# Four sums and three low parts moved from POOL to DVE at two stage boundaries, and the last stage's second g tile loaded a step ahead into kept buffers

## The chip, the cores and the metric

One Trainium2 chip, one core. The metric is device microseconds of one execution. The kernel before takes 1404.5 us, the median of three runs (1402.43 to 1406.67).

## The reference, cut to what matters

```python
# B, H, S, D = 8, 8, 576, 64; tokens = 4608
k_p, v_p = mean of k, v over 8 keys
attn = softmax(q @ k_p.T / sqrt(D)) @ v_p            # -> x [4608, 512]
h  = x @ w_in                                        # [4608, 1024]
ln = layernorm(h * softmax(h)) * g_ln
x2 = ln @ w_out                                      # [4608, 512]
g  = silu(x2 @ w2_in)                                # [4608, 2048]
out = g @ w2_out                                     # [4608, 512]
```

All data are float32 and the weights come as 8-byte words. A product is made from two parts of each factor, a high part (rounded to fp32r by ACT) and a low part (what is left, by a subtraction): high*high, high*low and low*high, so three matmuls for each one.

## The kernel before, in words

The work has three stages.

**Lead-in** (0 to about 640 us): attention and the first FFN, in 36 token tiles of 128. A script of letters (`STEP`, and `TAIL` for the last tiles) sets the order on PE. For a token tile, `hidden1` (L440) makes h in PSUM, `solu_max` (L451, DVE) takes the row maximum, `solu_norm` the exponentials (L458, ACT) and their product with h (L459, DVE; L462, POOL), `solu_scale` the squares (L468, ACT), a chain of one-column instructions (L469 to L474, POOL) and the normalised row `e` (L475, POOL). `norm_T` transposes `e` on PE (L490) and splits it into `lnh` (L123, ACT) and `lnl` (L124, DVE), and `project1` (L510) makes x2, which goes through ACT (L513) to DRAM.

**Second FFN, first product** (from 614 us; the last tiles of the lead-in run beside its first call): one level of Strassen, 7 products in place of 8. There are 12 steps n (6 groups of 768 tokens, twice, for the halves of w2_in's columns) with 4 calls `hidden2(n, i)` each. A call makes 7 products of 6 matmuls (L707), in the order L11, S2, S1, S3, L12, S4, L22, and ACT (L723, L727, L736, L677), DVE (L717) and POOL (L717) put them together into `gt`, which SP stores to DRAM (L678). Token sums `T1` to `T4` and the split of tokens are made by `tokens(n)` (sums by `sub`, L529; high parts L640, ACT; low parts L529, DVE), weight sums and splits of quarter q by `quad(q)` (first sum L554 and the others L529, DVE; high parts L565, ACT; low parts L529, on DVE or, where `lo` is given `pool`, on POOL). `tokens(0)` and `quad(0)` come from the background queue of the lead-in. The products of call (0, 0) land in PSUM tiles of the lead-in; the fifth and the sixth share one tile of two banks.

**Last stage** (from 1020.86 us): g @ w2_out, again Strassen. A g tile q is 512 tokens by 512 of g's columns (1 MB in two row halves, 36 of them); `load_g` (L801, SP) reads it, `sums_g` (L811 and L529, POOL) makes two sums, `prepare(m)` one operand (high part L830, ACT; low part L529, DVE) into a ring of 9, and `product2` (L853) one block of 12 matmuls, 7 blocks to a g tile. So blocks 0 to 6 need the first g tile, 7 to 13 the second, 14 to 20 the third. The weights of part u come by `load_part(u, j)` (L785), issued on ACT's queue: part 0 for blocks 0 to 6 and half of the next seven, part 1 for the other half, parts 2 and 3 at blocks 4 and 11.

From step n = 0 of the second stage on, ACT, DVE, POOL and SP run in the order of the program; before that only PE does, and a scheduler orders the others. `plan` hangs pieces on 28 slots of a step, one after each product. In step 11, slot 0 loads the first g tile, the slots 1 to 24 hold the loads of parts 0 and 1, slot 10 `sums_g(0)`, and 14 to 27 `prepare(0)` to `prepare(6)`. `finish_pair` stores a call's `gt` in the next call, and the last one after the step. A DMA also waits, on its issuing queue, until the DMA eight issues earlier in the program has landed, since the program uses eight DMA semaphores in turn.

Buffers: pools on the "left" side are a stack. `wx` (2 buffers of 4 KB a partition) holds quarter sums and, from step 2 to 10, row buffers of w2_out (`load_rows`); `wr` holds the raw quarters (`w2r`). `wq1`, `to` and `wx` are closed after step 11 (`bt.close()`), and `gr1`, `gr2` and others open in their place.

```python
    load_g(1)          # L1112, behind bt.close()
    load_g(2)
    ...
    sums_g(1, s_tmp)
    prepare(7)()
    prepare(8)()
```

Of the kernel before, what the change touches and what calls it, by code (L numbers as in the profile page):

```python
# [9 lines left out]
F32 = mybir.dt.float32  # L10
# [15 lines left out]
P = 128  # L26
# [14 lines left out]
GO = 512  # L41
# [41 lines left out]
def pooled_attention__solu__silu_kernel(  # L83
# [13 lines left out]
    nc = tc.nc  # L97
# [422 lines left out]
    pools = {}  # L520
# [14 lines left out]
    wq, w2r = {}, {}  # L535
# [36 lines left out]
    def quad(q):  # L572
        sum_, hi, lo, src = quarter(q)
        pool = nc.gpsimd
        return [
# [51 lines left out]
    def tokens(n):  # L627
# [22 lines left out]

        eng = nc.gpsimd
        work = [
# [136 lines left out]
    def load_g(q):  # L789
        c, s = divmod(q, NSET)  # L790
        if q % 3 == 0:
            raw = pools["x2r"].tile([P, 2, 2, GO], F32, tag="x2r", name="gr")
        else:
            raw = pools[f"gr{q % 3}"].tile([P, 2, 2, GO], F32, tag="gr", name="gr")
        done = 0
        while done < GO:
            g, o = divmod(c * GO + done, G2)
            m = min(GO - done, G2 - o)
            for h in range(2):
                f = h * FC2 // 2 + 2 * s  # L800
                nc.sync.dma_start(raw[:, h, :, done : done + m], gd[g][:, f : f + 2, o : o + m])  # L801
            done += m
        graw[q] = raw
# [3 lines left out]
    def sums_g(q, temps):  # L807
        raw = graw[q]
        a11, a21, a22 = raw[:, 0, :, :256], raw[:, 0, :, 256:], raw[:, 1, :, 256:]
        s1, s2 = (temps(k).rearrange("p (f d) -> p f d", d=256) for k in (1, 2))  # L810
# [4 lines left out]
    def prepare(n):  # L815

        q, j = divmod(n, 7)
        raw = graw[q]
        a11, a21, a12, a22 = (raw[:, i, :, 256 * k : 256 * k + 256] for i in range(2) for k in range(2))
        s1, s2 = sums[q]  # L820
# [225 lines left out]
    )  # L1046
    banks[:] = [0]
    open_pool("wq1", 1, "left", bt)
    open_pool("to", 1, "left", bt)
    open_pool("wx", 1, "left", bt)  # L1050
    ctx.enter_context(
# [8 lines left out]
    for n in range(N2):  # L1060
# [22 lines left out]
        if n == N2 - 1:  # L1083
# [5 lines left out]
            ]  # L1089
            work = [(0, lambda: load_g(0))]  # L1090
            for j in range(7):
                work += [(3 * j + 1, lambda j=j: load_part(0, j, early[j], nc.scalar)),
                         (3 * j + 6, lambda j=j: load_part(1, j, more[j], nc.scalar))]
            s0 = lambda k: pools["wx"].tile([P, 512], F32, tag=f"a{k - 1}", name="s")
            lows = {}
# [13 lines left out]
    bt.close()  # L1109
    for name in ("gr1", "gr2", "ob", "m2", "w2o"):  # L1110
        open_pool(name, 1, "left")
    load_g(1)  # L1112
    load_g(2)

# [65 lines left out]
```

## Time and profile before

| | |
|---|---|
| runs, us | 1406.67, 1404.5, 1402.43 (median 1404.5) |
| the profiled execution, us | 1403.74 |
| its span, us | 1402.0 |
| PE busy (matmuls) | 1294.8 us, 92% |
| DVE / ACT / POOL busy | 71% / 51% / 47% |
| mean DMA rate | 162 GB/s |
| chain that ended last, by engine | PE 49%, DVE 7%, issue 5%, DMA 4%, ACT 3%, POOL 2% |

The span is the time from the first to the last instruction that the profile shows, on the one core that runs; the execution's own time is 1.74 us longer. The profile gives each instruction its start and duration, and the idle time of its engine just before it with what ended that. In the stages PE is the engine that is nearly always busy, so what is to be looked for are the places where it is not.

### The profile page before, as it was taken

To read this page: it belongs to the slowest core of one execution; us is meant where nothing else is said; L and a number is where in the kernel's file an instruction comes from. 1 tells how busy PE (TensorE), PEld (TensorE's weight loads), DVE (VectorE), ACT (ScalarE), POOL (GpSimd) and SP (SyncE) were. 2 spreads that over 40 slices of the span, in tenths; PEclk is the share of its full clock that TensorE was granted. 3 is DMA by queue.
4 is the path that set the end of the run, shared out by engine and by line. 5 is a ranking of instruction groups with operands and counts; after the bars stand their busy time and mean duration, and the time that the engine had idled before them with its cause. 6 is when DMAs were issued, how large, how long until landed. Compare 5 with 4: busy or idle time off the path is not lost.

```text
span 1402.0 us, 23904 instructions
## 1 busy us (share of the span) xinstructions
PE 1294.8 (92%) x8712; PEld 1227.4 (88%) x8712; DVE 999.4 (71%) x1438; ACT 709.1 (51%) x1772; POOL 661.5 (47%) x829
## 2 busy tenths in 40 slices
PE   2589899999999999889998999999979999999998
PEld 2469789988989899789888988999979999999998
DVE  6896566766766565445787889888547788877785
ACT  4684555565555555343554555554433444434442
POOL 5674344444444433444555666777323333433332
PEclk7899999999999999999999999999989999999999
DMA  7655244543434211122566678665776344444431
GB/s 227 207 159 164 80 130 143 156 139 114 140 99 128 91 61 61 61 76 94 194 243 250 245 266 307 238 237 195 294 271 255 128 151 151 151 129 143 134 95 74
DMA packets 100550, 227.01 MB, mean 162 GB/s; under 512 B 8272, under 2 KB 29776, under 8 KB 98896
## 3 DMA queue, kind: packets, MB, share of 16 engines
q1 hardware_dynamic: 96400, 210.80, 45.1%
q10 hardware_dynamic: 4032, 14.68, 2.8%
q8 instruction: 69, 1.13, 0.3%
q14 instruction: 49, 0.40, 0.1%
HBM read 141.56 MB, written 83.89 MB: 161 GB/s over the span
## 4 chain that ended last, share of the span: by engine, by line
PE 49%; DVE 7%; issue 5%; DMA 4%; ACT 3%; POOL 2%; SPq 0%; ACTq 0%; DVEq 0%; POOLq 0%
PE op L853 24%; PE m L707 12%; PE xp L510 6%; PE hp L440 5%; DVE gt L717 2%; DVE wr L529 1%; PE tp L490 1%; DMA w2r<-w2if 1%; DVE t L529 1%; DVE u L717 1%; ACT gt L677 1%; DMA x2r<-x2d 1%; PE sp L311 1%; DMA w2o<-wod 1%; DVE w2r L529 1%
## 5 line engine op out<-in xcount | busy, mean ns | idle before, releaser
L707 PE MATMUL m<-t,w2s 128*128 128x384 f32 x2016 | 367.2, 340 | 23.9 <-DVE gt L717 11.8
L707 PEld LDWEIGHTS m<-t,w2s 128*128 128x128 f32 x2016 | 352.4, 190 | 38.3 <-DVE gt L717 14.6
L853 PE MATMUL op<-w2o,gt 128*128 128x256 f32 x3024 | 368.0, 284 | 8.5 <-ACT gt L830 7.9
L853 PEld LDWEIGHTS op<-w2o,gt 128*128 128x128 f32 x3024 | 366.0, 193 | 10.5 <-ACT gt L830 8.8
L529 DVE TENSOR_TENSOR gt<-gr,gt 128x512 fp32r<-128x512 f32 x180 | 164.7, 949 | 67.4 <-ACT gt L830 67.4
L830 ACT ACTIVATE gt<-gr 128x512 fp32r<-128x512 f32 x180 | 103.2, 623 | 151.4 <-DVE gr L529 132.5
L717 POOL TENSOR_TENSOR gt<-u,m 128x384 f32<-128x384 f32 x96 | 114.5, 1203 | 134.3 <-ACT m L727 91.8
L510 PE MATMUL xp<-lnh,w1oh 128*128 128x256 f32 x576 | 168.1, 292 | 0.5 <-ACT lnh L123 0.2
L510 PE MATMUL xp<-lnl,w1oh 128*128 128x256 f32 x576 | 163.9, 285 | 1.1 <-DVE lnl L124 1.1
L510 PE MATMUL xp<-lnh,w1ol 128*128 128x256 f32 x576 | 163.8, 284 | 0.0
L440 PE MATMUL hp<-w1ih,xTh 128*128 128x512 f32 x288 | 119.0, 413 | 8.9 <-DVE e L459 8.9
L736 ACT ACTIVATE gt<-gt 128x768 f32<-128x768 f32 x48 | 40.7, 847 | 157.2 <-DVE gt L717 157.2
L811 POOL TENSOR_TENSOR s<-gr 128x512 f32<-128x512 f32 x36 | 58.3, 1618 | 127.1 <-DVE gt L529 74.2
L329 ACT ACTIVATE pr<-sp,st 128x72 f32<-128x72 f32 x288 | 88.3, 330 | 56.8 <-POOL st L321 56.7
L440 PE MATMUL hp<-w1il,xTh 128*128 128x512 f32 x288 | 115.5, 401 | 0.6 <-POOL w1il L156 0.6
L440 PE MATMUL hp<-w1ih,xTl 128*128 128x512 f32 x288 | 115.7, 402 | 0.3 <-DVE xTl L124 0.3
L510 PEld LDWEIGHTS xp<-lnh,w1oh 128*128 128x128 f32 x576 | 111.4, 193 | 1.7 <-DVE lnl L124 0.7
L510 PEld LDWEIGHTS xp<-lnl,w1oh 128*128 128x128 f32 x576 | 111.6, 194 | 1.4 <-DVE lnl L124 1.3
L510 PEld LDWEIGHTS xp<-lnh,w1ol 128*128 128x128 f32 x576 | 111.3, 193 | 0.0
L529 DVE TENSOR_TENSOR t<-tt,t 128x768 fp32r<-128x768 f32 x48 | 64.8, 1354 | 14.1 <-ACT t L640 14.0
L440 PEld LDWEIGHTS hp<-w1ih,xTh 128*128 128x128 f32 x288 | 56.3, 196 | 21.1 <-issue 9.2
L830 ACT ACTIVATE gt<-s 128x512 fp32r<-128x512 f32 x72 | 42.1, 621 | 62.6 <-POOL s L529 56.6
(129 smaller groups left out, 2352.4 us busy)
## 6 DMA issues: line engine op xcount, KB each, us to landing
gd<-gt SPq DMA_DIRECT2D x48, 768.0 KB, 4.5
gr<-gd SPq DMA_DIRECT2D x48, 512.0 KB, 6.2
x2r<-x2d SPq DMA_DIRECT2D x12, 1536.0 KB, 7.6
wod<-wo SPq DMA_DIRECT2D x56, 256.0 KB, 2.7
gr<-gd SPq DMA_DIRECT2D x48, 256.0 KB, 5.4
q<-qT SPq DMA_DIRECT2D x36, 256.0 KB, 3.2
raw<-kT SPq DMA_DIRECT2D x32, 288.0 KB, 3.5
x2d<-xo SPq DMA_DIRECT2D x18, 512.0 KB, 3.4
```

The costliest lines, as they stand in the source:

```text
L311: nc.tensor.matmul(sp[done : done + n, p // 2, (p % 2) * 2 * SP : (p % 2 + 1) * 2 * SP], q[:, p, done : done + n], kbd[b % 2][:, p, :], st ...
L329: behind["ACT"] = nc.scalar.activation(pr[:, g, h], sv[:, g, h], AF.Exp, scale=SCALE, bias=st[:, 0, g, h : h + 1], accum_out=st[:, 1, g, h ...
L440: nc.tensor.matmul(hp[:, f], l, r, start=(n == 1 and m == 0), stop=(n == KC and m == 2))
L490: nc.tensor.transpose(tp[:, k * P : (k + 1) * P], e[:, f, k * P : (k + 1) * P], ident)
L510: nc.tensor.matmul(xp[:, :GW], l, r, start=(k == 0 and m == 0), stop=(k == FC1 - 1 and m == 2))
L529: eng.tensor_tensor(dst, a, b, op=ALU.subtract)
L707: nc.tensor.matmul(to, wt[:, a, o : o + P], tk[:, b, k], start=(k == 0 and m == 0), stop=(k == 1 and m == 2),)
L717: eng.tensor_tensor(dst, a, b, op=ALU.add)
L736: nc.scalar.activation(gt[:, 0], gt[:, 0], AF.Silu)
L811: nc.gpsimd.tensor_tensor(s1, a21, a22, op=ALU.add)
L830: nc.scalar.activation(ring[n][:, 0], src, AF.Copy)
L853: nc.tensor.matmul(op[:, 256 * h : 256 * h + 256], t[:, l, i, ts], w[:, r], start=(s == i == h == m == 0), stop=(s == NSET - 1 and i == h ...
```

## The change

It edits five things:

- `quad(0)`: the three low parts that were on POOL (of S1, L12 and L22) go to DVE. `quad(1)` stays.
- `tokens(0)`: the four sums T1 to T4 go from POOL to DVE. `tokens(n)` for the later n stays.
- `load_g(q)` with q % 3 == 1 uses the two buffers of `wx`, one for each row half, in place of a pool `gr1`. `wx` is opened below `wq1` and `to` and not closed. `load_g(1)` is now a piece of step 11, slot 10, where it stood behind `bt.close()`.
- The loads of part 1 (256 KB each) go from the slots 6, 9, ... 24 of step 11 to the slots 21 to 27.
- The two sums of the first g tile are kept in `wr` in place of `wx`.

```diff
     def quad(q):
         sum_, hi, lo, src = quarter(q)
-        pool = nc.gpsimd
+        pool = nc.gpsimd if q else nc.vector
...
-        eng = nc.gpsimd
+        eng = nc.gpsimd if n else nc.vector
         work = [
             (0, lambda: sub(eng, tmp(T1), r12, r11)), (4, lambda: sub(eng, tmp(T2), r22, t[T1])),
...
     def load_g(q):
         c, s = divmod(q, NSET)
-        if q % 3 == 0:
-            raw = pools["x2r"].tile([P, 2, 2, GO], F32, tag="x2r", name="gr")
+        if q % 3 == 1:
+            raw = [pools["wx"].tile([P, 2, GO], F32, tag=f"a{h}", name="gr") for h in range(2)]
         else:
-            raw = pools[f"gr{q % 3}"].tile([P, 2, 2, GO], F32, tag="gr", name="gr")
+            raw = pools["gr" if q % 3 else "x2r"].tile(
+                [P, 2, 2, GO], F32, tag="gr" if q % 3 else "x2r", name="gr")
+            raw = [raw[:, h] for h in range(2)]
...
-                nc.sync.dma_start(raw[:, h, :, done : done + m], gd[g][:, f : f + 2, o : o + m])
+                nc.sync.dma_start(raw[h][:, :, done : done + m], gd[g][:, f : f + 2, o : o + m])
...
+    open_pool("wx", 1, "left")
     open_pool("wq1", 1, "left", bt)
     open_pool("to", 1, "left", bt)
-    open_pool("wx", 1, "left", bt)
...
-            work = [(0, lambda: load_g(0))]
+            work = [(0, lambda: load_g(0)), (10, lambda: load_g(1))]
             for j in range(7):
                 work += [(3 * j + 1, lambda j=j: load_part(0, j, early[j], nc.scalar)),
-                         (3 * j + 6, lambda j=j: load_part(1, j, more[j], nc.scalar))]
-            s0 = lambda k: pools["wx"].tile([P, 512], F32, tag=f"a{k - 1}", name="s")
+                         (21 + j, lambda j=j: load_part(1, j, more[j], nc.scalar))]
+            s0 = lambda k: pools["wr"].tile([P, 512], F32, tag=f"w2r{k - 1}", name="s")
...
-    for name in ("gr1", "gr2", "ob", "m2", "w2o"):
+    for name in ("gr", "ob", "m2", "w2o"):
         open_pool(name, 1, "left")
-    load_g(1)
     load_g(2)
```

How it moves instructions, at three places. First POOL, at the end of the lead-in, with `solu_scale` of one token tile (L469 to L475) and the sums of `tokens(0)` (`tt<-x2r`). Before:

```order
L470 TENSOR_TENSOR ls<-ls 128x1
L471 TENSOR_SCALAR ls<-ls 128x1
L529 TENSOR_TENSOR tt<-x2r 128x768
L462 TENSOR_SCALAR ls<-ls 128x1
L529 TENSOR_TENSOR tt<-x2r,tt 128x768
L529 TENSOR_TENSOR tt<-x2r 128x768
L529 TENSOR_TENSOR tt<-x2r,tt 128x768
L472 TENSOR_SCALAR ls<-ls 128x1
L473 TENSOR_TENSOR ls<-ls,mhalf 128x1
L474 TENSOR_TENSOR ls<-ls 128x1
L475 TENSOR_SCALAR e<-e,ls 128x1024
```

Changed:

```order
L470 TENSOR_TENSOR ls<-ls 128x1
L471 TENSOR_SCALAR ls<-ls 128x1
L462 TENSOR_SCALAR ls<-ls 128x1
L472 TENSOR_SCALAR ls<-ls 128x1
L473 TENSOR_TENSOR ls<-ls,mhalf 128x1
L474 TENSOR_TENSOR ls<-ls 128x1
L475 TENSOR_SCALAR e<-e,ls 128x1024
```

The four sums are gone from between L471 and L472; on DVE they stand among the seven low parts of `tokens(0)`, between L459 of this tile and L451 of the next.

Second DVE, at the first call of `hidden2` (`u2`, `u3` and `gt` are its temporaries, L554 the first sum of quarter 1, `w2s` weight parts of quarter 0, the number behind it the buffer). Before:

```order
L529 TENSOR_TENSOR w2s5_6666<-wt_6643,w2s5_6666 128x512
L529 TENSOR_TENSOR w2s6_6674<-w2r_6608,w2s6_6674 128x512
L529 TENSOR_TENSOR w2s2_6681<-wt_6676,w2s2_6681 128x512
L717 TENSOR_TENSOR u2_6752<-m_6755,m1_6750 128x384
L554 TENSOR_TENSOR wt_6999<-w2r_6979 128x512
L717 TENSOR_TENSOR u3_6753<-m_6757,u2_6752 128x384
L717 TENSOR_TENSOR gt_6749<-m_6758,m1_6750 128x384
L717 TENSOR_TENSOR gt_6749<-m_6758,gt_6749 128x384
L717 TENSOR_TENSOR gt_6749<-m_6759,u3_6753 128x384
```

Changed:

```order
L529 TENSOR_TENSOR w2s6_6674<-w2r_6608,w2s6_6674 128x512
L529 TENSOR_TENSOR w2s1_6679<-w2r_6607,w2s1_6679 128x512
L529 TENSOR_TENSOR w2s2_6681<-wt_6676,w2s2_6681 128x512
L529 TENSOR_TENSOR w2s3_6720<-w2r_6608,w2s3_6720 128x512
L717 TENSOR_TENSOR u2_6752<-m_6755,m1_6750 128x384
L717 TENSOR_TENSOR u3_6753<-m_6757,u2_6752 128x384
L717 TENSOR_TENSOR gt_6749<-m_6758,m1_6750 128x384
L554 TENSOR_TENSOR wt_6999<-w2r_6979 128x512
L717 TENSOR_TENSOR gt_6749<-m_6758,gt_6749 128x384
L717 TENSOR_TENSOR gt_6749<-m_6759,u3_6753 128x384
```

The low parts of L12 and L22 (and that of S1, further up) have come in, and L554 has moved behind two more of the call's instructions.

Third SP's queue in step 11 and behind it (`gd5` the stores of g, `gr` loads of g tiles, one number for each buffer; 10590 is the first g tile). Before:

```order
L801 DMA gr_10590<-gd0_85 128x2x512 x2
L678 DMA gd5_90<-gt_10575 256x1x768
L678 DMA gd5_90<-gt_10647 256x1x768
L678 DMA gd5_90<-gt_10722 256x1x768
L678 DMA gd5_90<-gt_10804 256x1x768
L801 DMA gr_10905<-gd0_85 128x2x512 x2
L801 DMA gr_10908<-gd0_85 128x2x512 x2
```

Changed:

```order
L803 DMA gr_10590<-gd0_85 128x2x512 x2
L678 DMA gd5_90<-gt_10575 256x1x768
L803 DMA gr_10688<-gd0_85 128x2x512
L803 DMA gr_10689<-gd0_85 128x2x512
L678 DMA gd5_90<-gt_10646 256x1x768
L678 DMA gd5_90<-gt_10723 256x1x768
L678 DMA gd5_90<-gt_10803 256x1x768
L803 DMA gr_10905<-gd0_85 128x2x512 x2
```

The two halves of the second g tile (10688, 10689; before 10905) have moved past three of the step's stores; the third tile (10905) is the first load behind the last store.

## Rows read from the trace of the kernel before

**Rows 1.** The page of the profiled execution, its first line.

```profile
span 1402.0 us, 23904 instructions
```

**Rows 2.** Busy time by stretch of the span (`us` of the stretch, then busy us and instructions of each engine, the granted TensorE clock, the DMA share and GB/s): the stretch around the last token tiles of the lead-in and two around the start of the last stage.

```profile
550.00:600.00 50.00, 44.13 (x284) 40.39 (x283) 27.85 (x30) 20.64 (x37) 23.00 (x32) 0.93 0.12 43
1010.00:1020.00 10.00, 8.88 (x52) 8.56 (x51) 4.23 (x8) 4.12 (x7) 5.27 (x4) 1.00 1.03 415
1030.00:1040.00 10.00, 4.27 (x24) 3.84 (x23) 0.69 (x1) 0.63 (x1) 1.95 (x2) 0.72 0.91 314
```

**Rows 3.** Instructions of PE in order of time at the end of the lead-in (start us, us, engine, line, operation, out<-in, shape, count, and in brackets the idle time before and what ended it): the transposes of one token tile and the eighth matmul behind them, for an earlier tile and for the tile with the idle time, and the transposes of the next one.

```profile
552.25 1.03 PE L490 MATMUL tp<-ident,e 128*128 128x128 f32 x8
553.96 0.28 PE L510 MATMUL xp<-lnl,w1oh 128*128 128x256 f32 x1
570.38 1.97 PE L490 MATMUL tp<-ident,e 128*128 128x128 f32 x8 [5.87 <-POOL e L475]
573.63 0.28 PE L510 MATMUL xp<-lnl,w1oh 128*128 128x256 f32 x1
584.00 1.03 PE L490 MATMUL tp<-ident,e 128*128 128x128 f32 x8
```

**Rows 4.** Instructions of POOL in order of time there: the first of the four sums of `tokens(0)`, the first and the last of the four one-after-another instructions (L472 to L475) of `solu_scale` behind them, and the same two of the next tile.

```profile
555.99 1.85 POOL L529 TENSOR_TENSOR tt<-x2r 128x768 f32<-128x768 f32 x1
565.53 1.74 POOL L472 TENSOR_SCALAR ls<-ls 128x1 f32<-128x1 f32 x1
569.12 1.20 POOL L475 TENSOR_SCALAR e<-e,ls 128x1024 f32<-128x1024 f32 x1
578.38 0.27 POOL L472 TENSOR_SCALAR ls<-ls 128x1 f32<-128x1 f32 x1 [1.38 <-ACT sqd L468]
579.66 1.21 POOL L475 TENSOR_SCALAR e<-e,ls 128x1024 f32<-128x1024 f32 x1
```

**Rows 5.** Instructions of DVE in order of time: the first low part of `tokens(0)`, two low parts beside the third and fourth sum on POOL, the row maximum of the next tile, and one low part of the same shape at 994.9 us.

```profile
556.25 2.40 DVE L529 TENSOR_TENSOR t<-x2r,t 128x768 fp32r<-128x768 f32 x1
561.26 5.10 DVE L529 TENSOR_TENSOR t<-x2r,t 128x768 fp32r<-128x768 f32 x2
568.88 1.21 DVE L451 TENSOR_REDUCE ls<-hp 128x1 f32<-128x1024 f32 x1
...
994.90 0.94 DVE L529 TENSOR_TENSOR t<-tt,t 128x768 fp32r<-128x768 f32 x1
```

**Rows 6.** Instructions of ACT in order of time there: the squares of the tile, and the exponentials of the next one.

```profile
558.74 1.15 ACT L468 ACTIVATE sqd<-e,ls 128x1024 bf16<-128x1024 f32 x1
...
572.88 1.11 ACT L458 ACTIVATE e<-hp,ls 128x1024 f32<-128x1024 f32 x1
```

**Rows 7.** Instructions of PE in order of time: the 42 matmuls of the first `hidden2` call, and the first long row of the calls after it.

```profile
614.81 2.59 PE L707 MATMUL m<-t,w2s 128*128 128x384 f32 x14
618.29 3.07 PE L707 MATMUL m<-t,w2s 128*128 128x384 f32 x16 [0.90 <-POOL w2s L529]
624.84 3.89 PE L707 MATMUL m<-t,w2s 128*128 128x384 f32 x12 [3.48 <-DVE gt L717]
643.84 10.98 PE L707 MATMUL m<-t,w2s 128*128 128x384 f32 x62
```

**Rows 8.** DVE in that first call: the first sum of quarter 1 (L554), in order of time.

```profile
623.16 0.69 DVE L554 TENSOR_TENSOR wt<-w2r 128x512 f32<-128x512 f32 x1 [5.45 <-DMA w2r<-w2if]
```

**Rows 9.** Instructions of PE in order of time at the start of the last stage.

```profile
1020.86 10.61 PE L853 MATMUL op<-w2o,gt 128*128 128x256 f32 x84
1037.20 3.23 PE L853 MATMUL op<-w2o,gt 128*128 128x256 f32 x12 [5.73 <-ACT gt L830]
1041.32 9.07 PE L853 MATMUL op<-w2o,gt 128*128 128x256 f32 x60 [0.90 <-ACT gt L830]
1050.81 0.50 PE L853 MATMUL op<-w2o,gt 128*128 128x256 f32 x2 [0.42 <-ACT gt L830]
1051.54 10.09 PE L853 MATMUL op<-w2o,gt 128*128 128x256 f32 x82 [0.22 <-DVE gt L529]
1062.49 0.50 PE L853 MATMUL op<-w2o,gt 128*128 128x256 f32 x2 [0.86 <-ACT gt L830]
1063.22 17.05 PE L853 MATMUL op<-w2o,gt 128*128 128x256 f32 x140 [0.22 <-DVE gt L529]
```

**Rows 10.** Instructions of SP's DMA queue in order of time there (merged): the loads of g tiles from the second one on.

```profile
1030.54 35.80 SPq L801 DMA_DIRECT2D gr<-gd  x14
```

**Rows 11.** The last line of the view of one tile, from 990 to 1080 us for `gr` (the g tiles loaded) and from 985 to 1035 us for `gd` (the g stores and the loads from them).

```profile
DMA to landing us min/median/max: 6.0/7.9/14.3
...
DMA to landing us min/median/max: 3.7/7.6/15.5
```

**Rows 12.** Instructions of ACT in order of time at the start of the last stage.

```profile
1029.08 0.83 ACT L677 ACTIVATE gt<-gt 128x768 f32<-128x768 f32 x1
1036.52 0.63 ACT L830 ACTIVATE gt<-gr 128x512 fp32r<-128x512 f32 x1 [6.61 <-DMA gr<-gd]
1040.64 1.15 ACT L830 ACTIVATE gt<-s 128x512 fp32r<-128x512 f32 x2 [3.50 <-POOL s L529]
1046.36 3.67 ACTq L785 DMA_DIRECT2D w2o<-wod  x7
1050.13 1.15 ACT L830 ACTIVATE gt<-gr 128x512 fp32r<-128x512 f32 x2 [3.17 <-DMA w2o<-wod]
```

More of the change, by code (lines that the diff above doesn't have):

```diff
@@ L808, in sums_g @@
         raw = graw[q]
-        a11, a21, a22 = raw[:, 0, :, :256], raw[:, 0, :, 256:], raw[:, 1, :, 256:]
+        a11, a21, a22 = raw[0][:, :, :256], raw[0][:, :, 256:], raw[1][:, :, 256:]
         s1, s2 = (temps(k).rearrange("p (f d) -> p f d", d=256) for k in (1, 2))
@@ L818, in prepare @@
         raw = graw[q]
-        a11, a21, a12, a22 = (raw[:, i, :, 256 * k : 256 * k + 256] for i in range(2) for k in range(2))
+        a11, a21, a12, a22 = (raw[i][:, :, 256 * k : 256 * k + 256] for i in range(2) for k in range(2))
         s1, s2 = sums[q]
```

## The prediction, made before the changed kernel was run

> **What bounds the kernel now.** I began with the page: its first line gives a span of 1402.0 us [rows 1], and the profiled execution took 1403.74. PE is busy nearly everywhere, so the second view was busy time by stretch, to see where it is not [rows 2]: 44.1 of 50 us at 550 to 600, 4.3 of 10 at 1030 to 1040. In the same stretches the granted TensorE clock is 0.93 and 0.72, a mix of its two levels, 2.4 and 1.2 GHz. So an idle PE is paid for twice there: with the idle time and with slower matmuls behind it. The third view was PE in order of time at these and at the first calls of the second FFN, then the engine that each idle time names.
>
> Place one, end of the lead-in. PE waits 5.87 us for `e` (L475 on POOL) [rows 3]. POOL ran the four sums of `tokens(0)` from 555.99 to 565.53 and could only then begin with L472 [rows 4], though the squares were done at 559.9 [rows 6].
>
> Place two, the first `hidden2` call. Its 42 matmuls take from 614.81 to 628.73. PE waits 0.90 us for a low part from POOL and 3.48 us for DVE (L717) [rows 7]. DVE had stood for 5.45 us at L554, a sum of quarter 1 that nobody needs yet, until its load landed [rows 8].
>
> Place three, the start of the last stage. Blocks 0 to 6 run to 1031.47, and block 7 waits 5.73 us [rows 9] for an operand whose high part waited for the second g tile [rows 12]. That load was issued at 1030.54 [rows 10], behind the last store, whose silu ended at 1029.91 [rows 12].
>
> **The change part by part.**
>
> *Place one.* POOL loses four sums, DVE gains them. The new end of `e`: squares at 559.9 (ACT as before; it comes earlier if anything), then L472 to L475. Undisturbed these take 578.38 to 580.87, 2.5 us; beside DVE's instructions they took 565.53 to 570.32, 4.8 us [rows 4]. So `e` is there between 562.4 and 564.7, and PE, which arrives at 564.5, waits between 0 and 0.2 us; I allow 0.4. The slow clock goes with the idle time: transposes to eighth matmul took 3.25 us behind the stall and 1.71 us for the earlier tile [rows 3], so 1.5 us. Gain 5.9 - 0.4 + 1.5 = **7.0 us**.
>
> What DVE pays: eleven instructions of 768 columns instead of seven. Before, the first took 2.40 us and a pair 5.10, always beside a sum on POOL; the same shape with POOL out of the way took 0.94 [rows 5]. I take 0.94, the nearest row once POOL is idle: 11 x 0.94 = 10.3 us from 556.3, so the next row maximum (L451) starts at about 566.7, where it started at 568.88 [rows 5]. That is hidden beside PE's next matmuls. The other end, 2.55 us each, is a rival below.
>
> The Trainium skill ("SBUF — State Buffer", section "Who interferes with whom") says why it could be 0.94: a DVE instruction with two SBUF inputs and a GpSimd instruction that reads SBUF exclude each other, each for its whole length. The same rule speaks against the change, since the eleven can now hold up L472 to L475; if each of these four waited for one DVE instruction, `e` would come at 559.9 + 4 x 0.94 + 2.5 = 566.2 and the gain would be 5.7 us instead of 7.0.
>
> *Place two.* Three low parts go from POOL to DVE, in front of the call's instructions, and L554 goes behind two of these. A low part of 512 columns is two thirds of 768, so about 0.63 us; three make 1.9 us on DVE before the first L717. PE has five products to do before it needs anything of DVE but operands, so this is covered; if not, it is at most 1.9 us. 62 matmuls took 10.98 us, 0.177 each, in the calls behind [rows 7], so 42 take 7.4 us. The sixth product shares a PSUM tile with the fifth and still waits until DVE has read that: I put 0.7 us, the length of L554 with more columns [rows 8]. L554 may go on waiting for its load; only the last two L717 stand behind it, and PE goes on with the lead-in's transposes. Gain 13.9 - 7.4 - 0.7 = **5.8 us**, at least 3.9, at most 6.5.
>
> *Place three.* From 1020.86 to 1063.22 PE did 242 matmuls; at the 17.05 / 140 = 0.122 us of the row behind [rows 9] they take 29.5 us, so 12.9 us are lost. With the second tile loaded in step 11, its sums are made on POOL before the last silu, and block 7's operand needs only ACT's turn: silu to 1029.91, five more load issues than before in front of it (seven took 3.67 us [rows 12], so five take 2.6; ACT's gaps there hide a part, I take half), high part and low part together 0.68 us (1036.52 to 1037.20 [rows 9, 12]). Block 7 starts at about 1031.9, 0.4 us after PE is free. Next, the ring: from block 7's high part to block 13's took 13.6 us, 3.5 of it waiting for POOL's sums [rows 12], which are done now; 10.1 remain, with 3.67 us of issuing part 2. PE needs 8.8 us for those six blocks, so block 13 waits 1.3; behind the same queue the third tile's load and part 2 are close together, and an issue may wait for a landing, so I take 2.0. Block 20 has the same structure (part 3): 0.86 + 0.22 now, 2.0 taken. Left of 12.9: 4.4. Gain **8.5 us**, at most 12.4, and at least 1, since the last silu does not come earlier and the tile could land as late as now.
>
> Removed waits that cost nothing: `wx` was free in step 11, and the sums' new place, `wr`, has not been used since step 6. Memory traffic is the same 227 MB.
>
> Sum: 7.0 + 5.8 + 8.5 = 21.3 us, and 1403.74 - 21.3 = 1382.4. The median of the three runs is 0.8 above the profiled execution, so **1383 us**.
>
> **The rivals.**
>
> *The loads collide.* At 1010 to 1020 the DMA engines are already full (share 1.03, 415 GB/s) [rows 2], a g tile took up to 14.3 us to land and a store up to 15.5 [rows 11]. The added 1 MB stands ahead of three stores on SP's queue. At 415 GB/s it is worth 2.5 us; if the stores land that much later, the last silu follows, and with parts 2 and 3 also late by as much each, place three keeps 1.0 us. For it: the numbers. Against it: five of the seven part 1 loads, 1.3 MB, leave the same stretch. Total 7.0 + 5.8 + 1.0: **1391 us**. The Trainium skill ("DMA: Bandwidth & Descriptors", section "Issuing engines are not separate DMA queues") says that DMAs of different issuing engines share the same DMA engines and interleave; by that rule this rival is the nearer, as ACT's weights and SP's tile cannot help each other by standing on two queues.
>
> *POOL is starved.* If L472 to L475 get through only when DVE's eleven are done, `e` comes at 566.6 + 2.5 = 569.1 and place one keeps 1.3 us: **1389 us**. Against it: L472 took 1.74 us where it takes 0.27 alone [rows 4], so it came through between DVE's instructions.
>
> *DVE becomes the bound: the other side.* If its two-input instructions take 2.55 us for a reason other than POOL, ten of them put L451 at 581.8. From there to the next `e` it was 12.0 us (568.88 to 580.87), 2.8 of them because the exponentials started at 572.88, behind the late transposes, and not at 570.1 [rows 4 to 6]; so 9.2, and 1.6 more for the eleventh instruction among them: 592.6. PE came to these transposes at 584.00 without a wait [rows 3], and would come 7.0 earlier, at 577.0. So it would wait 15.6 us, and place one costs about 9 us more than now, quarter 0's parts at 1.7 us each take away place two and 2 more, and place three, whose DVE instructions have their own rows, gives 8.5 back: **1406 us**. The point: about 1.85 us each, where the same sum gives 584.0 and nothing is gained. Against it: 0.94 [rows 5].
>
> *More goes than I counted*: no wait at blocks 13 and 20 (+4): **1378 us**.
>
> **How the numbers follow.** Forecast 0.66, loads collide 0.17, POOL starved 0.06, DVE bound 0.03, more 0.08. The range 1376 to 1392 takes in the forecast with its bounds, the first two rivals and the last. No change means within 0.3%, about 4 us, which is what measurements of this kernel can tell: of 1383, 1391, 1389 and 1378 all lie outside it, the DVE rival within it or over it. Faster 0.94, same 0.04, slower 0.02.
>
> **What would show it.** Right: no idle PE in front of the transposes near 564; the 42 matmuls of the first call within 8 to 9 us; block 7 within 1.5 us of block 6, blocks 13 and 20 with 1 to 3 us each; DVE's sums and low parts at about 0.95 us. Wrong: PE still waiting for L475, or for L451's tile; a long wait of block 7 on a landing; stores that land after more than 16 us with DVE or POOL waiting for `gt` in step 11.

## The result, and the profile after

The changed kernel takes 1383.59 us (median of 4 runs, 1382.4 to 1385.07), the kernel before in the same runs 1404.12 (1402.43 to 1406.67). The ratio is 0.985, 95% interval 0.9826 to 0.9874, so 20.5 us less. The forecast was 1383. The profiled execution took 1382.4, its span is 1380.6.

Busy time by stretch of the changed kernel (columns as in [rows 2]). Here and in all rows after, L832, L855 and L813 stand for L830, L853 and L811 of before.

```profile
550.00:600.00 50.00, 49.39 (x319) 44.64 (x318) 26.95 (x39) 23.14 (x46) 18.91 (x33) 1.00 0.16 58
950.00:1000.00 50.00, 49.24 (x281) 48.28 (x280) 35.31 (x52) 24.57 (x44) 27.33 (x22) 1.00 0.66 248
1000.00:1050.00 50.00, 45.82 (x347) 44.80 (x346) 30.30 (x45) 21.46 (x37) 17.18 (x13) 0.97 1.01 375
1020.00:1030.00 10.00, 6.70 (x56) 6.50 (x54) 2.99 (x5) 2.59 (x5) 2.55 (x2) 1.00 1.04 399
1030.00:1040.00 10.00, 9.78 (x70) 9.57 (x70) 6.21 (x9) 3.32 (x7) 2.91 (x2) 0.83 1.03 372
1050.00:1060.00 10.00, 10.00 (x86) 10.00 (x85) 8.70 (x11) 3.31 (x6) 4.59 (x4) 1.00 0.02 6
```

At 550 to 600 PE is busy 49.39 us where it was 44.13 [rows 2]. At 1030 to 1040 it is busy 9.78 us where it was 4.27, but there the changed kernel is some 15 us further on in its work: its own longest wait falls into 1020 to 1030 (6.70). The DMA engines are full (share 1.01) from 1000 to 1050, had room before (0.66) and are empty behind it. The same stretch of the kernel before:

```profile
1000.00:1050.00 50.00, 42.13 (x269) 40.65 (x267) 20.70 (x32) 15.52 (x27) 14.88 (x12) 0.90 0.82 308
```

Counted from 20 us ahead of the last stage to 30 us into it, so at the same place of the work, the DMA share is 0.83 before (1000.86 to 1050.86) and 1.01 after (986.11 to 1036.11).

PE of the changed kernel in order of time at the three places; these rows answer to [rows 3, 7, 9].

```profile
566.73 1.10 PE L490 MATMUL tp<-ident,e 128*128 128x128 f32 x8 [0.61 <-POOL e L475]
...
609.68 5.37 PE L707 MATMUL m<-t,w2s 128*128 128x384 f32 x30
615.70 2.38 PE L707 MATMUL m<-t,w2s 128*128 128x384 f32 x12 [0.65 <-DVE gt L717]
...
1006.11 8.79 PE L855 MATMUL op<-w2o,gt 128*128 128x256 f32 x72
1015.25 0.51 PE L855 MATMUL op<-w2o,gt 128*128 128x256 f32 x2 [0.36 <-ACT gt L832]
1016.05 10.35 PE L855 MATMUL op<-w2o,gt 128*128 128x256 f32 x82 [0.29 <-DVE gt L529]
1029.71 0.51 PE L855 MATMUL op<-w2o,gt 128*128 128x256 f32 x2 [3.30 <-ACT gt L832]
1030.43 49.84 PE L855 MATMUL op<-w2o,gt 128*128 128x256 f32 x402 [0.22 <-DVE gt L529]
```

Place one: 0.61 us of idle time instead of 5.87. Place two: 609.68 to 618.08, 8.40 us for the 42 matmuls instead of 13.92, and one wait of 0.65. Place three: twelve matmuls are a block, so the 72 of the first row are blocks 0 to 5, and the waits stand at block 6 (0.36 and 0.29) and at block 13 (3.30 and 0.22). Block 7 waits for nothing, nor does block 20.

POOL, with L472 to L475 of the tile of place one [rows 4], and two instructions in step 11:

```profile
560.25 1.22 POOL L472 TENSOR_SCALAR ls<-ls 128x1 f32<-128x1 f32 x1 [1.38 <-ACT sqd L468]
561.55 1.15 POOL L473 TENSOR_TENSOR ls<-ls,mhalf 128x1 f32<-128x1 f32 x1
563.31 3.36 POOL L475 TENSOR_SCALAR e<-e,ls 128x1024 f32<-128x1024 f32 x1
...
1011.77 2.45 POOL L717 TENSOR_TENSOR gt<-u,m 128x384 f32<-128x384 f32 x2 [8.22 <-DMA gd<-gt]
```

DVE, with the first sum of `tokens(0)`, two of its low parts, the next row maximum [rows 5], and L554 in the first call [rows 8]:

```profile
557.86 0.95 DVE L529 TENSOR_TENSOR tt<-x2r 128x768 f32<-128x768 f32 x1
564.81 2.66 DVE L529 TENSOR_TENSOR t<-tt,t 128x768 fp32r<-128x768 f32 x2
567.40 1.21 DVE L451 TENSOR_REDUCE ls<-hp 128x1 f32<-128x1024 f32 x1
...
617.56 0.69 DVE L554 TENSOR_TENSOR wt<-w2r 128x512 f32<-128x512 f32 x1 [1.92 <-DMA w2r<-w2if]
```

ACT, with the squares [rows 6] and, at the start of the last stage [rows 12], the last silu, the seven issues of part 2 and the high part behind them:

```profile
558.90 1.15 ACT L468 ACTIVATE sqd<-e,ls 128x1024 bf16<-128x1024 f32 x1 [1.49 <-POOL ls L462]
...
1015.11 0.83 ACT L677 ACTIVATE gt<-gt 128x768 f32<-128x768 f32 x1
1022.65 6.27 ACTq L785 DMA_DIRECT2D w2o<-wod  x7
1029.03 1.15 ACT L832 ACTIVATE gt<-gr 128x512 fp32r<-128x512 f32 x2 [5.76 <-DMA w2o<-wod]
```

ACT stands at these seven issues for 6.27 us, and the high part of block 13 (1029.03) is behind them: that is the 3.30 us of PE. The sixth and the seventh issue stood until an earlier load had landed: they began at 1025.58 and 1028.60, and the landings are at 1025.56 and 1028.58.

To see what belongs to the change and what to one run, I cut every profile at five instructions that all kernels have: DVE's row maximum L451 number 31 and number 36 (of the 36 tiles), ACT's silu L677 of calls 2 and 44 (of 48), and the last addition on DVE. "Place one" is from the first to the second, "place two" from there to the silu of call 2, "between" up to the silu of call 44, and "place three" from there to the end. The stretches in us come from one profile each; every ratio is against runs of the kernel before on the same chip. The labels are those of the experiments below.

| kernel | place one | place two | between | place three | median | ratio to before, 95% |
|---|---|---|---|---|---|---|
| before | 67.78 | 53.67 | 336.41 | 401.74 | 1404.12 | |
| e1_sums | 61.04 | 53.73 | 335.13 | 402.28 | 1396.23 | 0.9939 (0.9917 to 0.9962) |
| e2_lows | 68.32 | 48.13 | 332.42 | 402.46 | 1398.59 | 0.9963 (0.9948 to 0.9978) |
| e7_l554_later | 68.20 | 49.32 | 336.34 | 403.09 | 1400.09 | 0.9974 (0.996 to 0.9988) |
| e3_loads | 67.84 | 53.65 | 335.29 | 395.49 | 1396.08 | 0.9937 (0.992 to 0.9955) |
| changed | 61.03 | 48.15 | 333.72 | 393.74 | 1383.59 | 0.985 (0.9826 to 0.9874) |
| e11_changed_again | 61.04 | 48.14 | 334.02 | 395.07 | 1382.01 | 0.9838 (0.9818 to 0.9859) |
| e8_two_sums_back | 66.17 | 48.13 | 337.35 | 393.83 | 1386.61 | 0.9886 (0.9863 to 0.991) |
| e4_part1_old_slots | 61.05 | 48.11 | 333.83 | 396.17 | 1384.76 | 0.9871 (0.9848 to 0.9894) |
| e10_tile_late | 61.03 | 48.14 | 335.85 | 401.52 | 1388.23 | 0.9882 (0.9863 to 0.99) |
| e5_part2_on_sp | 61.04 | 48.13 | 334.71 | 395.68 | 1384.82 | 0.9873 (0.9849 to 0.9897) |
| e6_part2_spread | 61.04 | 48.14 | 333.69 | 396.79 | 1385.04 | 0.9872 (0.985 to 0.9894) |
| e9_part2_only_on_sp | 61.04 | 48.12 | 332.58 | 396.22 | 1382.15 | 0.9845 (0.9823 to 0.9866) |
| e12_part3_behind_tile4 | 61.04 | 48.14 | 336.50 | 393.34 | 1382.89 | 0.9845 (0.9824 to 0.9867) |

With the changed code places one and two repeat to a few hundredths (61.03 to 61.05 in nine profiles, 48.11 to 48.15 in ten); with the old code place one is 67.8 to 68.3. "Between" runs from 332.4 to 337.4 with no order in it, so the 2.7 us that the changed kernel's profile has there against that of before can't be put down to the change. Place three with the loads of before is 401.7 to 403.1, with the changed loads 393.7 to 395.5, so differences of a microsecond say nothing there. Part of that spread is the clock: over the 10 us from 1027 to 1037 of e11_changed_again, behind block 13's wait, the granted clock is 0.66, where the changed kernel's first profile has 0.83 from 1030 to 1040, and its place three is 1.3 us longer with the same code.

### The profile page after: what moved, and what is told of

Read it like the earlier page. It is cut to its first block, busy times and chain, and to the rows that moved or that the text cites. A ratio compares the mean times of both kernels' runs of the same rounds, so it can differ in the third digit from the quotient of the medians.

```text
span 1380.6 us, 23898 instructions
## 1 busy us (share of the span) xinstructions
PE 1288.1 (93%) x8712; PEld 1222.4 (89%) x8712; DVE 997.2 (72%) x1445; ACT 708.3 (51%) x1772; POOL 650.9 (47%) x822
## 4 chain that ended last, share of the span: by engine, by line
PE 49%; DVE 7%; issue 4%; DMA 4%; ACT 3%; POOL 1%; SPq 0%; DVEq 0%; ACTq 0%; POOLq 0%
PE op L855 25%; PE m L707 11%; PE xp L510 6%; PE hp L440 5%; DVE gt L717 2%; DMA w2r<-w2if 1%; DMA gd<-gt 1%; DVE wr L529 1%; PE tp L490 1%; DVE u L717 1%; DVE t L529 1%; DMA x2r<-x2d 1%; ACT gt L677 1%; DVE wo L529 1%; PE sp L311 1%
## 5 line engine op out<-in xcount | busy, mean ns | idle before, releaser
L707 PE MATMUL m<-t,w2s 128*128 128x384 f32 x2016 | 362.6, 338 | 18.8 <-DVE gt L717 7.3
L855 PE MATMUL op<-w2o,gt 128*128 128x256 f32 x3024 | 365.7, 284 | 4.2 <-ACT gt L832 3.7
L855 PEld LDWEIGHTS op<-w2o,gt 128*128 128x128 f32 x3024 | 364.6, 193 | 5.2 <-ACT gt L832 4.1
L832 ACT ACTIVATE gt<-gr 128x512 fp32r<-128x512 f32 x180 | 103.4, 623 | 145.3 <-DVE gr L529 129.4
L717 POOL TENSOR_TENSOR gt<-u,m 128x384 f32<-128x384 f32 x96 | 115.5, 1213 | 128.3 <-ACT m L727 84.1
L813 POOL TENSOR_TENSOR s<-gr 128x512 f32<-128x512 f32 x36 | 56.6, 1574 | 118.7 <-DMA gr<-gd 62.6
L832 ACT ACTIVATE gt<-s 128x512 fp32r<-128x512 f32 x72 | 42.2, 622 | 58.3 <-POOL s L529 56.1
```

The source lines that it names most:

```text
L707: nc.tensor.matmul(to, wt[:, a, o : o + P], tk[:, b, k], start=(k == 0 and m == 0), stop=(k == 1 and m == 2),)
L717: eng.tensor_tensor(dst, a, b, op=ALU.add)
L813: nc.gpsimd.tensor_tensor(s1, a21, a22, op=ALU.add)
L832: nc.scalar.activation(ring[n][:, 0], src, AF.Copy)
L855: nc.tensor.matmul(op[:, 256 * h : 256 * h + 256], t[:, l, i, ts], w[:, r], start=(s == i == h == m == 0), stop=(s == NSET - 1 and i == h ...
```

## The experiments

**One part at a time.** e1_sums: the sums of `tokens(0)` alone.

```diff
-        eng = nc.gpsimd
+        eng = nc.gpsimd if n else nc.vector
```

> The kernel before with one edit: the four sums of tokens(0) on DVE. If the three places are independent (the prediction's sum): PE's idle time before the late transposes falls from 5.87 to about 0.6 us, the DVE instructions beside an idle POOL take 0.95 us, the first hidden2 call still takes 13.9 us and the start of the last stage still loses 12.9; about 6.7 us in all, 1397.4. If the idle time is only handed on (the load that L554 waits for lands at the same time as before): the first call grows to about 20 us and the total stays within 1402 to 1405. If DVE's instructions were slow for a reason of their own: 2.4 us each and a total above 1404.

It took 1396.23 us. PE:

```profile
566.35 1.09 PE L490 MATMUL tp<-ident,e 128*128 128x128 f32 x8 [0.61 <-POOL e L475]
...
612.78 3.08 PE L707 MATMUL m<-t,w2s 128*128 128x384 f32 x16 [0.89 <-POOL w2s L529]
619.38 3.91 PE L707 MATMUL m<-t,w2s 128*128 128x384 f32 x12 [3.53 <-DVE gt L717]
```

Place one has the 0.61 us of the full change, and place two keeps both its waits. DVE's sums took 0.95 us each. The first reading holds; the idle time is not handed on, and the load that L554 waits for lands earlier with all the rest.

e2_lows: the low parts of `quad(0)` alone.

```diff
-        pool = nc.gpsimd
+        pool = nc.gpsimd if q else nc.vector
```

> The kernel before with one edit: the three low parts of quad(0) on DVE, by which L554 also moves behind two more L717. If the order of L554 carries most of the gain: the first hidden2 call takes 8.4 us instead of 13.9, both waits (0.90 and 3.48) are gone but for about 0.65, total about 1398.6. If only the low parts on POOL counted: 0.9 us, and PE still waits about 3.5 us for an L717, total about 1403. If DVE is late with its three added instructions: a wait for w2s on DVE of up to 1.9 us in front of products 5 to 7.

1398.59 us. PE:

```profile
571.63 1.97 PE L490 MATMUL tp<-ident,e 128*128 128x128 f32 x8 [5.85 <-POOL e L475]
...
622.63 2.37 PE L707 MATMUL m<-t,w2s 128*128 128x384 f32 x12 [0.65 <-DVE gt L717]
```

Place one as before, place two as in the full change. e7_l554_later takes the two effects of this edit apart.

```diff
-            plan(n, [(7 + at, f) for at, f in quad(1)])
+            plan(n, [(8 + at, f) for at, f in quad(1)])
```

> The kernel before with one edit: quad(1) is planned one slot later, so that L554 stands behind all L717 of the first hidden2 call; the low parts of quad(0) stay on POOL. If the order of L554 is what costs 3.48 us: that wait goes, the wait of 0.90 for a low part on POOL stays, the call takes about 10 us, total about 1400.3. If POOL's low parts were the cause behind it: PE waits as long for something else, the call takes 13 us or more, total 1403 to 1405.

1400.09 us. PE:

```profile
618.24 3.07 PE L707 MATMUL m<-t,w2s 128*128 128x384 f32 x16 [0.90 <-POOL w2s L529]
621.96 2.38 PE L707 MATMUL m<-t,w2s 128*128 128x384 f32 x12 [0.65 <-DVE gt L717]
```

The wait of 0.90 for POOL is still there, the 3.48 became 0.65, and place two is 49.32: of the 5.5 us of place two, 4.35 come from the order of L554 and 1.2 from the low parts. Most of it was thus to be had without moving any work between engines. (e7 moves L554 further than the change does, behind all five L717 of the call, and the other pieces of quarter 1 by one slot with it.)

e3_loads: the changed kernel without the two DVE edits.

```diff
-        pool = nc.gpsimd if q else nc.vector
+        pool = nc.gpsimd
-        eng = nc.gpsimd if n else nc.vector
+        eng = nc.gpsimd
```

> The changed kernel without its two DVE parts: only the loads differ from the kernel before (second g tile in step 11 in kept buffers, part 1 at slots 21 to 27). If place three stands by itself: step 11 ends 1 to 1.5 us earlier, block 7 does not wait, block 13 waits 3.3 us and block 20 nothing, so 7 to 9 us less, 1395 to 1397. If the earlier gains had helped it (by moving loads against each other): less than 5 us, above 1399.

1396.08 us; block 7 does not wait, block 13 a little longer than expected:

```profile
1044.15 36.11 PE L855 MATMUL op<-w2o,gt 128*128 128x256 f32 x279 [4.29 <-ACT gt L832]
```

Against the median of before in the same runs (1403.59), the three parts alone give 7.4, 5.0 and 7.5 us, 19.9 together, and the full change 20.5: they add up, within what the intervals allow.

**Inside place one.** e8_two_sums_back: two of the four sums on POOL again.

```diff
-            (0, lambda: sub(eng, tmp(T1), r12, r11)), (4, lambda: sub(eng, tmp(T2), r22, t[T1])),
+            (0, lambda: sub(nc.gpsimd, tmp(T1), r12, r11)), (4, lambda: sub(nc.gpsimd, tmp(T2), r22, t[T1])),
```

> The changed kernel with the first two of the four sums of tokens(0) back on POOL, the other two on DVE. If POOL and DVE hold each other up: DVE's instructions beside these two sums take 1.9 to 2.6 us each and those behind them 0.95, the chain L472 to L475 starts only when the two sums are done (about 561) and PE waits 1.5 to 3 us, 1384 to 1386. If only POOL's own queue counted: DVE's instructions take 0.95 throughout, L472 starts at 561 and PE waits about 1 us, 1383 to 1384.

1386.61 us, above both expectations. DVE first, then POOL's two sums and PE:

```profile
556.46 2.40 DVE L529 TENSOR_TENSOR tt<-x2r 128x768 f32<-128x768 f32 x1
558.78 0.94 DVE L529 TENSOR_TENSOR t<-x2r,t 128x768 fp32r<-128x768 f32 x1
559.65 2.61 DVE L529 TENSOR_TENSOR t<-tt,t 128x768 fp32r<-128x768 f32 x1
```

```profile
556.20 1.84 POOL L529 TENSOR_TENSOR tt<-x2r 128x768 f32<-128x768 f32 x1
...
558.87 2.57 POOL L529 TENSOR_TENSOR tt<-x2r,tt 128x768 f32<-128x768 f32 x1
```

```profile
567.76 1.97 PE L490 MATMUL tp<-ident,e 128*128 128x128 f32 x8 [3.04 <-POOL e L475]
```

POOL ran the first sum from 556.20 to 558.04 and the second, 2.57 us long, from 558.87 to 561.44. DVE's first instruction began after the first sum and ended 0.82 us after it, the third the same with the second sum; the one between took 0.94, and there it was the sum that was long. So DVE's 2.4 us belong to POOL's company and not to the instruction. With 3.04 us of waiting and slow transposes behind it (1.97 us), place one loses 5.1 of its 7 us.

**Inside place three.** The loads' edit has two halves. e4_part1_old_slots undoes the move of part 1, e10_tile_late the early tile.

```diff
-                         (21 + j, lambda j=j: load_part(1, j, more[j], nc.scalar))]
+                         (3 * j + 6, lambda j=j: load_part(1, j, more[j], nc.scalar))]
```

> The changed kernel with the part 1 loads back at the slots 6, 9, ... 24 of step 11. If their move is what keeps step 11 free (the added g tile and part 1 collide in the DMA engines, 400 GB/s from 1000 on): the last stage starts 1.5 to 3 us later than in the changed kernel, 1385 to 1387. If the bytes only have to be moved before block 13 and the engines have room before 1000 us: the stage starts at most 0.5 us later and block 13 waits 1 us instead of 3.3, 1380 to 1383.

1384.76 us. PE:

```profile
1006.79 4.21 PE L707 MATMUL m<-t,w2s 128*128 128x384 f32 x12 [3.05 <-DVE gt L717]
1010.79 19.66 PE L855 MATMUL op<-w2o,gt 128*128 128x256 f32 x156
...
1031.34 0.50 PE L855 MATMUL op<-w2o,gt 128*128 128x256 f32 x2 [0.88 <-ACT gt L832]
```

With both loads early, step 11 stops for 3.05 us (the changed kernel has no such wait) and the stage starts at 1010.79 instead of 1006.11; block 13 then waits 0.88 instead of 3.30, since part 1's bytes are done. The wait in step 11 came by ACT: an issue of a weight load stood there until 1004.54, and half of the second g tile landed at 1004.52; the high part behind it was late by that, then DVE, then PE. Both expectations named a half of this. From the silu of call 44 to the last stage it is 29.0 us here, 23.9 in the changed kernel and 25.3 in that of before. Place three is 396.17, 0.7 to 2.4 us longer than with both halves.

```diff
-            work = [(0, lambda: load_g(0)), (10, lambda: load_g(1))]
+            work = [(0, lambda: load_g(0))]
...
+    load_g(1)
     load_g(2)
```

> The changed kernel with the second g tile loaded behind the last store again (in the kept buffers), while part 1 stays at slots 21 to 27. If the early tile is what place three gains by: block 7 waits 5 to 8 us again for a landing, with part 1 now loading beside it, and the total is 1388 to 1392. If the move of part 1 gave the gain and the tile little: a wait below 2 us, 1383 to 1385.

1388.23 us, and block 7 waits 7.19:

```profile
1021.23 3.23 PE L855 MATMUL op<-w2o,gt 128*128 128x256 f32 x12 [7.19 <-ACT gt L832]
```

So in place three, neither half: 402.4 (mean of the four kernels that have the loads of before); part 1 moved alone: 401.5; the tile alone: 396.2; both: 394.5 (mean of changed, e3, e8, e11). The tile gives 6 to 7 us. The move of part 1 gives one or two by this sum, which is no more than the spread of place three, and the whole times do not tell the changed kernel from e4 (0.985 and 0.9871, with intervals that overlap). What does repeat is step 11: from the silu of call 44 to the last stage it is 23.9 us in e10, as in the changed kernel, and 25.3 to 26.6 in the four kernels with the loads of before.

**What block 13 waits for.** ACT stands at part 2's issues. Four orders of the same loads were tried, against the changed kernel itself, run again:

> The changed kernel itself, once more, on the same chip as the two others: 1382 to 1385, block 13 waits 3.3 us, place one 0.61 and the first hidden2 call takes 8.4 us, if its profile was an ordinary one.

1382.01 us, with 3.39 at block 13, 0.61 in place one and 8.39 for the first `hidden2` call. First the issues on SP (e5_part2_on_sp):

```diff
-                load_part(u, k, w, nc.scalar)
+                load_part(u, k, w, nc.sync)
```

> The changed kernel with the loads of parts 2 and 3 issued on SP's queue instead of ACT's. If block 13 waits because ACT stands at the issues (6.3 us for seven, 1022.65 to 1028.92) and not because data is late: the 3.30 us and the low clock behind them go, 1379 to 1380. If the DMA engines are the bound there (399 GB/s at 1020 to 1040): the wait moves to the matmuls of block 14 or 15, which then wait for part 2 or for the third g tile, 3 us or more, 1383 or above.

1384.82 us. PE:

```profile
1016.23 23.86 PE L855 MATMUL op<-w2o,gt 128*128 128x256 f32 x192 [0.31 <-DVE gt L529]
...
1052.57 5.97 PE L855 MATMUL op<-w2o,gt 128*128 128x256 f32 x36 [2.17 <-ACT m L876]
1059.60 1.66 PE L855 MATMUL op<-w2o,gt 128*128 128x256 f32 x12 [1.06 <-ACT gt L832]
1062.13 18.11 PE L855 MATMUL op<-w2o,gt 128*128 128x256 f32 x147 [0.87 <-DVE ob L872]
```

Block 13's wait is gone, and so is block 14's: part 2 came in time. The wait came back at blocks 29 to 33 (block 29 is matmul 348), in all 4.1 us: its PSUM tile waited for L876 (the copy of a product out of PSUM) on ACT, which stood behind POOL's sums of g tile 4 (the fifth), whose load SP had issued behind part 3. The expectation had not seen that queue. (The two expectations that speak of "near block 26" mean this wait; I had miscounted.)

One issue behind each block (e6_part2_spread):

```diff
-        if n in (4, 11):
-            u = 2 + n // 11
-            for k in range(7):
-                w = pools["w2o"].tile([P, 2, 2, 256], F32R, tag=f"w{u}{k}", name="w2o")
-                load_part(u, k, w, nc.scalar)
+        if 1 <= n < 15:
+            u, k = 2 + (n - 1) // 7, (n - 1) % 7
+            w = pools["w2o"].tile([P, 2, 2, 256], F32R, tag=f"w{u}{k}", name="w2o")
+            load_part(u, k, w, nc.scalar)
```

> The changed kernel with one load of part 2 behind each of the blocks 1 to 7 and one of part 3 behind each of 8 to 14, on ACT's queue as before, in place of seven behind block 4 and seven behind block 11. If seven issues in a row on ACT are the cause: each stands before one operand, at most about 1 us each, block 13 does not wait, 1379 to 1381. If issues wait for landings because the engines are full: the operands of blocks 10 to 16 come late one by one and the same 3 to 4 us are spread over more waits, 1382 to 1385.

1385.04 us, near the second reading, but not spread as it has it: small waits at several blocks and a long one at block 17.

```profile
1035.62 0.50 PE L855 MATMUL op<-w2o,gt 128*128 128x256 f32 x2 [3.50 <-ACT gt L832]
```

Part 2 on SP and part 3 on ACT (e9_part2_only_on_sp):

```diff
-                load_part(u, k, w, nc.scalar)
+                load_part(u, k, w, nc.sync if u == 2 else nc.scalar)
```

> The changed kernel with the loads of part 2 alone on SP's queue; part 3 stays on ACT. With both on SP the wait at block 13 was gone and the time came back near block 26, where g tile 4 had been issued behind part 3 (SP's g loads at 1036.13 after seven issues of 8.07 us). If that reading holds: no wait at block 13 and none at 25 to 27, 3 to 4 us below the changed kernel, 1379.5 to 1380.5. If the DMA engines were the bound and not the order of the queue: waits of 3 us or more at blocks 20 to 27 again, 1383 to 1385.

1382.15 us, which is the changed kernel's time and not 3 to 4 us less; the first reading failed, and the wait that the second one named is there. PE, then ACT:

```profile
1013.58 20.44 PE L855 MATMUL op<-w2o,gt 128*128 128x256 f32 x166 [0.31 <-DVE gt L529]
1038.04 0.50 PE L855 MATMUL op<-w2o,gt 128*128 128x256 f32 x2 [4.02 <-ACT gt L832]
```

```profile
1030.50 6.75 ACTq L785 DMA_DIRECT2D w2o<-wod  x7
1037.36 1.15 ACT L832 ACTIVATE gt<-gr 128x512 fp32r<-128x512 f32 x2 [6.24 <-DMA w2o<-wod]
```

The same picture as at block 13, now at block 20 and part 3. Last, both on SP, part 3 behind the g tiles (e12_part3_behind_tile4):

```diff
-        if n in (4, 11):
-            u = 2 + n // 11
+        if n in (4, 13):
+            u = 2 + n // 13
...
-                load_part(u, k, w, nc.scalar)
+                load_part(u, k, w, nc.sync)
```

> The changed kernel with parts 2 and 3 on SP's queue, part 3 now behind block 13 and so behind the loads of g tiles 3 and 4. So far one wait of 3.3 to 4.1 us stayed, whichever queue had the loads: at block 13 (both on ACT), near block 26 (both on SP), at block 20 (one on each). If it is the order of the issues (something needed soon stands behind something needed late): no wait over 1 us at blocks 13 to 27, about 3.5 us below the changed kernel, ratio to before about 0.982, 1378 to 1380. If it is the bytes (DMA engines full from 1000 to about 1048 at 400 GB/s): 3 to 4 us of waits for w2o at blocks 21 to 27, ratio about 0.985, 1382 to 1385.

1382.89 us. PE, then busy time by stretch:

```profile
1017.32 21.87 PE L855 MATMUL op<-w2o,gt 128*128 128x256 f32 x178 [0.31 <-DVE gt L529]
1042.08 38.19 PE L855 MATMUL op<-w2o,gt 128*128 128x256 f32 x304 [2.90 <-DMA w2o<-wod]
```

```profile
1030.00:1040.00 10.00, 9.19 (x77) 8.98 (x75) 5.27 (x9) 2.98 (x6) 2.57 (x2) 1.00 1.05 385
1040.00:1050.00 10.00, 7.92 (x54) 7.95 (x55) 7.78 (x12) 5.46 (x10) 2.90 (x2) 0.83 1.03 394
```

Now PE itself waits 2.90 us at block 21, for a piece of part 3 that has not landed. Five orders, 2.9 to 4.1 us of waiting in one place each (at blocks 13, 29 to 33, 17, 20 and 21), and DMA engines that are full or nearly so (share 0.95 to 1.01 from 1000 to 1050): these runs fit that what is left in place three goes with the bytes that have to come there, not with the queue they are issued on. That is argued, not shown. A kernel that moves fewer bytes there, or some of them before 990 us (share 0.66 from 950 to 1000, of which the last 10 us have 1.04), was not tried, and neither was one in which more than eight DMAs may be on their way: at blocks 13 and 20 the wait came from an issue that stood until an earlier load had landed. No version that beats the changed kernel came out.

## Why the prediction was right, point by point

**Place one: 7.0 us forecast, 6.75 in the pair of profiles, 7.0 against the mean of the four kernels that have its old code.** The idle time was to be 0.4 at most and is 0.61. DVE's 0.94 was right (0.95), and the next row maximum came in time. One step inside it was wrong: the chain L472 to L475 was to take at most the 4.8 us that it took beside DVE before; it took 6.42 (560.25 to 566.67), L475 alone 3.36. The row was misread as an upper bound: L475 ran there from 569.12 to 570.32 beside the row maximum L451 (568.88 to 570.09, one input, in PSUM) and took 1.20, as it does alone [rows 4, 5]; only the first three of the four stood beside subtractions. In the changed kernel all four do. The error was covered by the squares, which POOL's shorter queue let end 1.45 us earlier (560.05 here, less 1.6 us by which this profile's lead-in was later, against 559.9). I had put that as "earlier if anything" and counted nothing for it. The Trainium skill ("SBUF — State Buffer", section "Who interferes with whom") has it that a DVE instruction with two SBUF inputs contends with a GpSimd (POOL) instruction that reads SBUF, over a shared port pair that is an exclusive lock. With one DVE instruction waited for by each of the four, the forecast had worked out 6.3 us for the chain; the trace agrees with that sum better than with the row I took, but not with its parts: the four were held up by 0.95, 0.60, 0.24 and 2.15 us against the tile of [rows 4], not by 0.94 each. The last two low parts on DVE, 2.66 us instead of 1.8, show the same from the other side.

**Place two: 5.8 forecast, 5.5 measured.** The call takes 8.40 where 8.1 were forecast, with one wait of 0.65 where I put 0.7. L554 still waits (1.92 us) with only the last two L717 behind it. The price of each half, not split in the forecast, is 4.35 for the order of L554 (e7) and 1.2 for the low parts (the rest of e2).

**Place three: 8.5 forecast, 8.0 in the pair of profiles, 7.9 between the means.** The sign and the mechanism were right: block 7 no longer waits for a landing (e10 brings 7.19 us of it back). The terms inside were mis-sized and partly cancel: block 7 was to wait 0.4 and block 6 waits 0.65 instead; block 13 was to wait 2.0 and waits 3.30, and 0.22 after its first two matmuls; the slow clock behind such a wait, which place one counts with 1.5 us, was put at nothing here and costs some 1.7 (clock 0.83 from 1030 to 1040; blocks 13 and 14 take 4.80 us with that 0.22, two later ones 2.88); block 20 was to wait 2.0 and does not; and step 11 itself became shorter by 1.4 us (the stage starts 14.75 earlier than before, the silu of call 44 13.35), where I had expected nothing. So of the 12.9 us of the stage 6.4 are left, where 4.4 were forecast (the same 242 matmuls take 35.85 us), and step 11 gives back 1.4. The term of block 13's wait, "3.67 us of issuing part 2" and 0.7 for a landing, was mis-sized: the seven issues took 6.27 us, with the engines full (share 1.04).

**The rivals.** "The loads collide" did not happen as priced: POOL stood 8.22 us in step 11 for a store, and a g tile took up to 18.1 us to land (14.3 before [rows 11]), but the stores of the step landed after at most 14.6 us (15.5 before), and PE did not wait in that step. The last line of the view of `gr`, 985 to 1035 us of the changed kernel:

```profile
DMA to landing us min/median/max: 6.2/7.3/18.1
```

The rival's germ is true, though: the DMA engines are full in this stretch now, and e4 shows the collision (3.05 us in step 11) as soon as part 1 is put back. The Trainium skill ("DMA: Bandwidth & Descriptors", section "Issuing engines are not separate DMA queues") says that DMAs started by different engines run on the same DMA engines and interleave. e5, e9 and e12 agree: another queue changed the place of the wait and not the time by more than the intervals tell (ratios 0.9873, 0.9845 and 0.9845, the changed kernel 0.985 and 0.9838). "POOL is starved" came half true in the length of the chain, and cost 0.61 us. "DVE becomes the bound" failed at its condition: 0.95 us, not 1.85. (By that rival's own sum, with the eleventh instruction counted as at 2.55, nothing is gained from 1.77 us on.) "More goes than I counted" came true at block 20 and not at block 13 (its 4 us less make 1379, not 1378).

So the parts were each within 0.6 us, but that is in part luck: inside places one and three, errors of 1 to 2 us cancelled. The two spans differ by 21.4, and 20.3 of that are the three places: "between" adds 2.7 and the lead-in takes 1.6 away (its tile 31 came at 539.35 instead of 537.74), and neither can be put down to the change.

## What to carry to other kernels

When an engine with a queue in order waits for a load that nobody needs yet, look at who stands behind it: moving L554, and what belongs to it, was worth 4.35 us, the work taken off POOL beside it 1.2. When a load is brought forward, ask next how full the DMA engines are over the whole stretch up to its last use. Here there were holes before (share 0.82), and a new order gained; with the holes gone (1.01 after), four more orders of the loads only chose where the wait stands. An instruction's duration beside one neighbour is not its duration: read it with the other engine idle as well before pricing a move, and look up which instruction of the neighbour each row stood beside.

## What was not expected of the hardware

POOL's one-column instructions are held up too, not only the long ones: L472 took 1.22 us beside DVE's two-input instructions and 0.27 alone [rows 4], and L475 3.36 instead of 1.21. And the hold goes by turns, not by a common slow-down: eight of DVE's 128x768 subtractions at place one (four before, one in the changed kernel, three in e8) were held up by an instruction of POOL, and each ended 0.81 or 0.82 us after that one, whether it took 1.79 us in all or 2.61.
